# Retention attention with a token mixer on one core: another order of the work on all engines, other places for the scalings of v, and a last tile in halves

## The chip, the cores and the metric

The kernel runs on one core of a Trainium2 chip. A core has five engines that run side by side, each through its own list of instructions in order: TensorE (PE, matmuls, with its weight loads shown as PEld), VectorE (DVE), ScalarE (ACT), GpSimd (POOL) and SyncE (SP). They wait for each other by semaphores. Transfers are issued from SyncE's and GpSimd's lists and carried out by 16 DMA engines. Matmuls read SBUF and write PSUM, which here is used as eight banks; DVE and ACT carry results from PSUM to SBUF.

The metric is the device time of one execution in microseconds. Four runs of the kernel before gave 98.87, 99.43, 99.64 and 100.15, with a median of 99.54.

## The reference, cut to what matters

Four batches, eight heads, 768 positions, 64 features a head. The first stage is a causal attention without softmax, with a decay `lam` of its own for each head; the second mixes tokens and ends in a projection.

```python
for b in range(nb):                      # 12 blocks of 64 positions
    intra = (qb @ kb.T * Dmask) @ vb     # Dmask[i, j] = lam ** (i - j) for i >= j, else 0
    inter = (qb * lam_pow) @ kv_state    # lam_pow = lam ** (pos + 1)
    out[:, :, sl] = intra + inter
    kv_state = lam ** 64 * kv_state + (kb * rev_pow).T @ vb
x = out                                  # as (4, 768, 512), heads side by side
wq, wk = x @ w_q, x @ w_k                # 512 -> 64 each
W_tok = (wq @ wk.T) / 8                  # 768 x 768 for each batch
y = relu(W_tok @ x) @ w_out              # (4, 768, 512), float32
```

Inputs and output are float32; the kernel computes in bfloat16 with float32 sums in PSUM.

## The kernel before

The work is cut into 16 pairs of heads, n = 4 * batch + pair, and each pair into six chunks of 128 positions. As the decay is a power, it is split: q is multiplied by lam to the position (`Dq`), v is divided by it (`DvI`), and the mask is then a plain triangle.

The steps of a pair, by the names in the order string: q, k, v are loaded by GpSimd's queue, one transfer of 192 KB (as written) for each, with a cast (L111 to L121). `sv` scales v in place, on DVE (`:v`) or on GpSimd (`:p`) (L236). `Aq` and `Ak` transpose q and k on TensorE (L246, L257), twelve transposes each; `eq` brings q back with its decay on DVE, `ek` brings k back on DVE or ACT. `S0` and `S1` are the scores of three chunks each (L272). `M0` and `M1` multiply them by the mask on DVE, from PSUM; in their place `Mc` copies them on ACT and `Mm` masks the copy in SBUF on DVE. `P` makes the states between chunks (L314): for n under 6 in their whole form, where TensorE adds all earlier chunks into each state and `G` is one copy; for the others in a shorter form, where DVE adds in three instructions. `I` applies the states to q, `V` the masked scores to v, into the same banks. `ex` brings the result to `xnat`, `F` transposes it, `ef` (or two `eg`) brings that to `xT`.

When the four pairs of a batch are done, its mix follows: `Q` projects (or `Qp`, one pair at a time), `eQ` copies, `K` (or `Kh`) transposes and `eK` (`ek2`) copies, `Y` multiplies wk with x, `YA`, `YB`, `YC` copy, `m` applies wq, `em` (or two `eh`) takes the relu, `O` is the output projection of a tile of 128 tokens (four matmuls of 128x512), and `eo` copies that tile to one of 12 buffers and has SyncE store it. `Z.c` is c matmuls on a block of zeros, which nothing reads (L526); nine of them stand ahead of all.

```
    for word in ORDER.split():
        piece, _, eng = word.partition(":")
        piece, *banks = piece.split("@")
        name, *at = piece.split(".")
```

The order string (from L29) is all the planning that runs: the scheduler of the framework is off, and each engine's list is the words that fall to it, in the order of the string. `S0.5@2` is the scores of pair 5 into banks 2 and 3; `:a`, `:v` and `:p` name the engine. The string opens with GpSimd's words: its loads and its scalings. `hold.14` makes SyncE wait for k of pair 14 before it stores anything, so the stores do not meet most of the loads.

Of the kernel before, what the change touches and what calls it, by code (L numbers as in the profile page):

```python
# [9 lines left out]
BF16 = mybir.dt.bfloat16  # L10
F32 = mybir.dt.float32
ALU = mybir.AluOpType
ACT = mybir.ActivationFunctionType

B, H, S, D = 4, 8, 768, 64
CH = 128
NCH = S // CH
HD = H * D
DHY = 64
NP = H // 2  # L20
HALF = 3 * CH
N = B * NP
WHOLE = 6
# [6 lines left out]
q.2 k.2 v.2 q.3 k.3 v.3 wq.0 wk.0 q.4 k.4 v.4 wo.0 q.5 k.5 v.5 q.6 k.6 v.6 q.7 k.7 v.7 sv.4:p q.8  # L30
k.8 v.8 sv.5:p q.9 k.9 v.9 q.10 k.10 v.10 sv.7:p q.11 k.11 v.11 q.12 k.12 v.12 sv.9:p q.13 k.13
v.13 sv.10:p q.14 k.14 v.14 sv.11:p q.15 k.15 v.15 sv.12:p sv.13:p sv.14:p hold.14 Aq.0@0 dq.2
eq.0@0 dq.3 Z.5@7 Ak.0@0 dq.1 ek.0@0:v Z.3@7 S1.0@0 sv.0:v S0.0@2 Mc.0@2 M1.0@0 Z.3@7 P.0@4 Aq.1@5
G.0@4:a Mm.0:v Z.1@7 I.0@0 eq.1@5 Ak.1@4 V.0@0 ek.1@4:v ex.0@0:a S0.1@4 sv.1:v S1.1@2 Mc.1@4 Z.1@7
F.0@0 M1.1@2 P.1@1 ef.0@0:a Aq.2@4 Mm.1:v G.1@1:a eq.2@4 Z.1@7 Ak.2@0 I.1@2 ek.2@0:v V.1@2 S1.2@0
sv.2:v ex.1@2:a S0.2@4 Mc.2@4 M1.2@0 Z.3@7 P.2@2 Aq.3@3 G.2@2:a Mm.2:v F.1@4 eq.3@3 Ak.3@2
ef.1@4:v I.2@0 V.2@0 ek.3@2:v ex.2@0:a sv.3:v Z.1@7 S0.3@2 S1.3@4 cw.0:a M1.3@4 Mc.3@2 Z.2@7 P.3@0
Qp.0.0@1 F.2@6 G.3@0:a Mm.3:v Qp.0.1@1 ef.2@6:a I.3@4 V.3@4 Qp.1.0@0 ex.3@4:a Aq.4@6 Ak.4@7 eq.4@6
F.3@4 ek.4@7:a Qp.1.1@0 Qp.0.2@1 eg.3.0@4:v Qp.1.2@0 eg.3.1@4:v Qp.0.3@1 eQ.0.0@1:v Qp.1.3@0
S1.4@4 eQ.0.1@0:a Kh.0.0@1 M1.4@4 ek2.0.0@1:a Kh.0.1@0 S0.4@6 ek2.0.1@0:a M0.4@6 Y.0@0 YA.0@0:a  # L40
YB.0@0:v Aq.5@1 YC.0@0:a m.0.1@6@7 eq.5@1 m.0.0@4@5 eh.0.1.0@6:a eh.0.0.0@4:v eh.0.0.1@5:a Ak.5@1
eh.0.1.1@7:a m.0.2@4@6 ek.5@1:v m.0.3@5@0 eh.0.2.1@6:a eh.0.3.1@0:v S0.5@2 eh.0.3.0@5:a S1.5@6
eh.0.2.0@4:v P.4@0 O.0.5@5 G.4@0:v M1.5@6 I.4@0 eo.0.5@5:a V.4@0 M0.5@2 Aq.6@4 ex.4@0:a Ak.6@5
eq.6@4 O.0.4@6 ek.6@5:a sv.6:v S1.6@4 S0.6@0 M1.6@4 F.4@7 O.0.3@2 ef.4@7:a M0.6@0 P.5@3 eo.0.3@2:a
Ak.7@7 G.5@3:v Aq.7@0 ek.7@7:a P.6@2 eq.7@0 I.5@4 V.5@4 G.6@2:v S0.7@0 ex.5@4:a eo.0.4@6:v Aq.8@7
M0.7@0 I.6@2 S1.7@4 O.0.0@6 eq.8@7 M1.7@4 V.6@2 eo.0.0@6:a O.0.2@7 ex.6@2:a sv.8:v P.7@6
eo.0.2@7:a Ak.8@2 G.7@6:v P.8@3 ek.8@2:a F.5@7 G.8@3:v Aq.9@6 ef.5@7:a Ak.9@2 eq.9@6 S1.8@4
ek.9@2:a S0.8@0 I.7@6 M1.8@4 V.7@6 F.6@2 ex.7@6:a M0.8@0 O.0.1@3 ef.6@2:v F.7@6 eo.0.1@3:a Aq.10@7
ef.7@6:v S0.9@2 eq.10@7 S1.9@0 Ak.10@6 M1.9@0 Q.1.0@7 ek.10@6:a M0.9@2 Q.1.1@4 eQ.1.0@7:a I.8@6
eQ.1.1@4:a S1.10@0 P.9@5 M1.10@0 K.1@4 V.8@6 eK.1@4:a G.9@5:v Aq.11@2 ex.8@6:a Y.1@4 eq.11@2  # L50
Ak.11@5 YA.1@4:a YB.1@4:v S0.10@2 ek.11@5:v YC.1@4:a m.1.0@6 M0.10@2 em.1.0@6:a m.1.1@0 Aq.12@5
P.10@4 em.1.1@0:a eq.12@5 m.1.3@2 I.9@6 G.10@4:v em.1.3@2:a V.9@6 m.1.2@0 ex.9@6:v I.10@4
em.1.2@0:a F.8@2 V.10@4 ef.8@2:v S0.11@0 ex.10@4:a S1.11@6 M0.11@0 O.1.1@2 M1.11@6 F.9@3
eo.1.1@2:a O.1.0@0 ef.9@3:a Ak.12@2 eo.1.0@0:a P.11@3 ek.12@2:v Ak.13@1 Aq.13@0 G.11@3:v ek.13@1:a
S1.12@6 S0.12@4 eq.13@0 I.11@2 V.11@2 M0.12@4 O.1.4@0 ex.11@2:a M1.12@6 F.10@1 eo.1.4@0:a F.11@2
ef.10@1:a S0.13@6 ef.11@2:v S1.13@4 Ak.14@0 M1.13@4 P.13@1 ek.14@0:a Aq.14@2 G.13@1:v Q.2.0@3
eq.14@2 Q.2.1@0 eQ.2.0@3:a M0.13@6 S1.14@2 eQ.2.1@0:a I.13@4 O.1.5@1 M1.14@2 V.13@4 sv.15:v
eo.1.5@1:a P.14@0 ex.13@4:a Aq.15@2 G.14@0:v K.2@1 Ak.15@3 eK.2@1:a P.12@4 eq.15@2 P.15@0
ek.15@3:a Y.2@1 G.12@4:v G.15@0:v S0.14@4 YB.2@1:a S0.15@2 I.12@6 YA.2@1:a M0.14@4 V.12@6 YC.2@1:a
O.1.2@0 ex.12@6:a M0.15@2 S1.15@4 eo.1.2@0:a I.14@6 m.2.1@2 M1.15@4 F.12@1 em.2.1@2:a V.14@6  # L60
ef.12@1:a I.15@4 ex.14@6:v m.2.2@2 V.15@4 em.2.2@2:a F.13@0 ex.15@4:v F.14@1 ef.13@0:a m.2.0@2
m.2.3@6 ef.14@1:v F.15@4 em.2.0@2:a O.1.3@0 ef.15@4:v em.2.3@6:a Q.3.0@1 eo.1.3@0:a Q.3.1@6
eQ.3.0@1:a O.2.0@0 eQ.3.1@6:v K.3@1 eo.2.0@0:v O.2.4@6 eK.3@1:a Y.3@7 eo.2.4@6:a O.2.3@6 YA.3@7:v
YB.3@7:v YC.3@7:v m.3.1@0 eo.2.3@6:a O.2.2@4 em.3.1@0:a m.3.0@6 eo.2.2@4:a m.3.2@2 m.3.3@0
em.3.0@6:v O.2.5@5 em.3.2@2:a em.3.3@0:a O.2.1@4 eo.2.5@5:v O.3.0@0 eo.2.1@4:a O.3.2@1 eo.3.0@0:v
O.3.4@4 eo.3.2@1:a O.3.3@5 eo.3.4@4:v O.3.1@1 eo.3.3@5:a O.3.5@0 eo.3.1@1:a eo.3.5@0:a
# [4 lines left out]
def kernel(  # L71
# [11 lines left out]
    nc = tc.nc  # L83
# [73 lines left out]
    blank = consts.tile([128, HD], BF16, name="blank")  # L157
# [75 lines left out]
    def copy(eng, to, of):  # L233
        return (nc.scalar.copy if eng == "a" else nc.vector.tensor_copy)(out=to, in_=of)  # L234
# [28 lines left out]

    def turned_q(n, o):
        qT[n] = tsb.tile([128, S], BF16, tag="qT", name="qT")
        nc.vector.tensor_tensor(out=qT[n], in0=PSH[:, o, 0:S], in1=Dq[n % NP], op=ALU.mult)  # L266
# [33 lines left out]
    def whole(n):  # L300
        return n < WHOLE


    def drawn(n, o):
        pr[n, 0] = tsb.tile([128, 2, HALF], BF16, tag="pr0", name="pr")
        nc.scalar.copy(out=pr[n, 0], in_=PS[:, o : o + 2, 0:HALF])

    def masked_late(n, eng):
        of = pr[n, 0].rearrange("j l (c i) -> j l c i", c=3)
        (nc.gpsimd if eng == "p" else nc.vector).tensor_tensor(  # L310
            out=of, in0=of, in1=mask2, op=ALU.mult
        )

    def states(n, o):  # L314
        to = PS[:, o, 0 : (NCH - 1) * D].rearrange("e (c f) -> e c f", c=NCH - 1)
        for c in range(NCH - 1):
            end = 2 if c < 2 and not whole(n) else NCH - 1
            for hl in range(2):
                mm(  # L319
                    to[R[hl], c:end, :],  # L320
                    fk[n][:, hl, c, :],
                    vn[n][:, hl, c, :].unsqueeze(1).to_broadcast([128, end - c, D]),
                    start=(c == 0),
                    stop=(c == NCH - 2),
                    skip_group_check=True,
                )

    def summed(n, o, eng):
        gs[n] = tsb.tile([128, NCH - 1, D], BF16, tag="gs", name="gs")
        of = PS[:, o, 0 : (NCH - 1) * D].rearrange("e (c f) -> e c f", c=NCH - 1)  # L330
        if whole(n):
            copy(eng, gs[n], of)
            return
# [186 lines left out]

    held = consts.tile([1, D], BF16, name="held")
# [3 lines left out]

    def zeros(count, o):  # L526
        for _ in range(count):
            mm(PS[:, o, :], blank[:, 0:128], blank, start=True, stop=True)  # L528
# [6 lines left out]
        sv=scale_v, Aq=turn_q, Ak=turn_k, eq=turned_q, ek=turned_k, S0=scores(0), S1=scores(1),  # L535
        M0=masked(0), M1=masked(1), Mc=drawn, Mm=masked_late, P=states, G=summed, I=inter, V=values, ex=attended, F=flip,
# [39 lines left out]
```

## Time and profile before

| | us |
|---|---|
| median of four runs | 99.54 |
| profiled execution, its time | 99.35 |
| its span, first to last instruction | 97.6 |
| TensorE busy | 89.8 |
| DVE busy | 72.4 |
| ACT busy | 61.5 |
| GpSimd busy, issues of its transfers included | 61.5 |
| first matmul of pair 3's k | 18.94 |
| landing of the last load, v of pair 15 | 67.36 |
| start of the last tile's matmuls, O.3.5 | 92.50 |
| issue and landing of the last store | 94.22, 96.27 |

Rows of digits on the page cut the span into 40 slices of 2.44 us; a digit is the busy share in tenths. A row of the chain gives a start, a duration, and what ran. In a row of the timeline the brackets tell how long the engine was idle before it and what ended that. The granted clock of TensorE was 1.00 from 5.9 us on. Landings are read from the trace's record of each transfer's semaphore, and the starts of the pieces by laying the trace's matmuls, in order, against the order string (all 1469 are in the trace).

### The profile page before, as it was taken

How to read it: one execution, taken by the hardware profiler on the slowest of the kernel's cores; microseconds unless marked ns; L12 is line 12 of the kernel's file. 1: busy time of each engine (PE TensorE's matmuls, PEld its weight loads, DVE VectorE, ACT ScalarE, POOL GpSimd, SP SyncE). 2: the span in 40 equal slices, each digit the busy share in tenths (PEclk: the TensorE clock that was granted, in tenths of full speed). 3: DMA queues.
4: the chain of work that ended last, by engine and by line, in shares of the span. 5: the costliest groups of instructions: out<-in, count | busy, mean ns of one | idle time of the engine just before them, and what ended most of it. 6: DMA issues, size and time to landing. Idle time of an engine off the chain costs nothing.

```text
span 97.6 us, 3425 instructions
## 1 busy us (share of the span) xinstructions
PE 89.8 (92%) x1469; PEld 56.6 (58%) x1469; DVE 72.4 (74%) x140; ACT 61.5 (63%) x101; POOL 61.5 (63%) x65
## 2 busy tenths in 40 slices
PE   5999899899989999999899999999999999999930
PEld 1354666667555657677657685776696764434400
DVE  5738798893889999998798699689999835554200
ACT  5576294378548458379557596775589992593440
POOL 5999999599579999999999999980000000000000
PEclk9999999999999999999999999999999999999999
DMA  0999999999999999999999999999970202545782
GB/s 1 97 145 160 163 158 168 157 163 191 186 165 161 168 160 166 165 160 166 168 167 160 166 164 161 167 188 376 380 287 11 108 7 108 215 169 213 284 307 102
DMA packets 67438, 16.60 MB, mean 170 GB/s; under 512 B 63840, under 2 KB 64352, under 8 KB 67424
## 3 DMA queue, kind: packets, MB, share of 16 engines
q0 software_dynamic: 63792, 10.10, 140.1%
q1 hardware_dynamic: 3632, 6.30, 17.1%
q8 instruction: 11, 0.18, 0.7%
q14 instruction: 3, 0.02, 0.1%
HBM read 20.19 MB, written 6.29 MB: 271 GB/s over the span
## 4 chain that ended last, share of the span: by engine, by line
PE 69%; POOL 10%; DMA 8%; DVE 4%; ACT 3%; issue 2%; POOLq 0%; ACTq 0%
PE ps L508 22%; DMA fk<-in_k_dram 8%; PE ps L359 6%; PE ps L277 6%; PE ps L382 5%; PE ps L260 5%; PE ps L319 5%; PE ps L404 4%; PE ps L251 4%; POOL fq L113 3%; PE ps L455 3%; POOL fk L117 3%; POOL fv L121 3%; PE ps L347 3%; PE ps L479 2%
## 5 line engine op out<-in xcount | busy, mean ns | idle before, releaser
L291 DVE TENSOR_TENSOR pr<-ps,mask 128x768 bf16<-128x768 f32 x28 | 26.0, 950 | 0.8 <-PE ps L277 0.7
L508 PE MATMUL ps<-wo,rmT 128*128 128x512 bf16 x96 | 23.6, 380 | 0.0
L117 POOL DMA_DIRECT2D fk<-in_k_dram x16 | 16.7, 1041 | 1.4 <-DMA wo<-in_moe_w_out_dram 1.4
L234 ACT COPY osb<-ps 128x512 f32<-128x512 f32 x19 | 11.2, 589 | 10.0 <-PE ps L508 9.8
L121 POOL DMA_DIRECT2D fv<-in_v_dram x16 | 16.7, 1046 | 0.3 <-issue 0.3
L234 ACT CAST xnat<-ps 128x768 bf16<-128x768 f32 x13 | 10.4, 800 | 7.2 <-PE ps L359 6.9
L113 POOL DMA_DIRECT2D fq<-in_q_dram x16 | 14.1, 880 | 1.3 <-POOLq L560 0.8
L239 POOL TENSOR_TENSOR fv<-fv,DvI 128x768 bf16<-128x768 bf16 x9 | 13.4, 1506 | 0.0
L508 PEld LDWEIGHTS <-rmT 128*128 128x128 bf16 x96 | 8.3, 98 | 8.6 <-issue 0.7
L528 PE MATMUL ps<-blank 128*128 128x512 bf16 x29 | 9.9, 460 | 1.2 <-DVE blank L158 1.2
L266 DVE TENSOR_TENSOR qT<-ps,dq 128x768 bf16<-128x768 bf16 x16 | 8.9, 554 | 2.7 <-PE ps L251 2.4
L490 ACT ACTIVATE rmT<-ps 128x768 bf16<-128x768 f32 (+1 forms) x16 | 10.6, 721 | 0.2
L277 PE MATMUL ps<-qT,kT 64*128 64x128 bf16 x192 | 9.0, 218 | 0.4 <-DVE kT L234 0.3
L234 ACT COPY kT<-ps 128x768 bf16<-128x768 bf16 x9 | 7.2, 800 | 2.9 <-PE ps L260 2.4
L359 PE MATMUL ps<-fv,pr 128*128 128x64 bf16 x192 | 8.5, 194 | 0.5 <-issue 0.5
L260 PE MATMUL ps<-ident,fk 128*64 128x128 bf16 x192 | 8.3, 221 | 0.6 <-DMA fk<-in_k_dram 0.5
L251 PE MATMUL ps<-ident,fq 128*64 128x128 bf16 x192 | 8.6, 227 | 0.1
L319 PE MATMUL ps<-fv,fk 128*64 128x128 bf16 (+4 forms) x160 | 8.0, 229 | 0.0
L277 PEld LDWEIGHTS <-kT 64*128 64x128 bf16 x192 | 5.6, 94 | 4.0 <-DVE kT L234 1.4
L382 PE MATMUL ps<-order,xnat 128*128 128x128 bf16 x96 | 7.8, 220 | 0.0
L359 PEld LDWEIGHTS <-pr 128*128 128x128 bf16 x192 | 6.8, 98 | 1.8 <-issue 0.8
L260 PEld LDWEIGHTS <-fk 128*64 128x64 bf16 x192 | 6.2, 110 | 2.6 <-DMA fk<-in_k_dram 1.2
(68 smaller groups left out, 130.6 us busy)
## 6 DMA issues: line engine op xcount, KB each, us to landing
out_dram<-osb SPq DMA_DIRECT2D x24, 256.0 KB, 2.0
fq<-in_q_dram POOLq DMA_DIRECT2D x16, 192.0 KB, 7.5
fk<-in_k_dram POOLq DMA_DIRECT2D x16, 192.0 KB, 8.0
fv<-in_v_dram POOLq DMA_DIRECT2D x16, 192.0 KB, 8.1
wo<-in_moe_w_out_dram POOLq DMA_DIRECT2D x1, 512.0 KB, 8.8
wqk<-in_moe_w_q_dram POOLq DMA_DIRECT2D x1, 64.0 KB, 7.2
wqk<-in_moe_w_k_dram POOLq DMA_DIRECT2D x1, 64.0 KB, 6.9
lam_all<-in_lam_dram SPq DMA_DIRECT2D x1, 4.0 KB, 2.5
```

Of the source, the lines that this page charges most:

```text
L113: nc.gpsimd.dma_start(out=fq[n], in_=rows_q(n))
L117: nc.gpsimd.dma_start(out=fk[n], in_=rows(n, k))
L121: nc.gpsimd.dma_start(out=fv[n], in_=rows(n, v))
L234: return (nc.scalar.copy if eng == "a" else nc.vector.tensor_copy)(out=to, in_=of)
L239: (nc.gpsimd if eng == "p" else nc.vector).tensor_tensor(out=vn[n], in0=fv[n], in1=DvI[:, 2 * kk : 2 * kk + 2, :].unsqueeze(3).to_broadcas ...
L260: nc.tensor.transpose(PSH[R[hl], o, c * CH : (c + 1) * CH], fk[n][:, hl, c, :], ident)
L277: mm(PS[:, o + hl, cc * CH : (cc + 1) * CH], kT[n][R[hl], c], qT[n][R[hl], c], start=True, stop=True, skip_group_check=True,)
L291: nc.vector.tensor_tensor(out=pr[n, a].rearrange("j l (c i) -> j l c i", c=3), in0=PS[:, o : o + 2, 0:HALF].rearrange("j l (c i) -> j l c ...
L319: mm(to[R[hl], c:end, :], fk[n][:, hl, c, :], vn[n][:, hl, c, :].unsqueeze(1).to_broadcast([128, end - c, D]), start=(c == 0), stop=(c == ...
L359: mm(PS[:, o + hl, c * D : (c + 1) * D], pr[n, c // 3][:, hl, (c % 3) * CH : (c % 3 + 1) * CH], vn[n][:, hl, c, :], start=False, stop=(c = ...
L382: nc.tensor.transpose(PSH[:, o, c * CH : (c + 1) * CH], xnat[b][:, c, kk * CH : (kk + 1) * CH], order,)
L508: mm(PS[:, o, :], rmT[b][:, kt].rearrange("f n i -> f (n i)")[:, t * CH : (t + 1) * CH], wo[:, kt, :], start=(kt == 0), stop=(kt == 3),)
```

## The change

It has five parts.

1. The order string is another one, for all engines. On TensorE pieces of several pairs stand closer together: for example Ak.15 and Aq.15 come ahead of S0.13, and four O of batch 0 stand between Y.1 and the m of batch 1. Evacuations change engine: DVE copies 14 output tiles instead of 5, ACT 9 instead of 19.
2. GpSimd's list: `wo`, the transfer of the output weights (512 KB as written), moves from behind v.4 to behind k.10. Eleven v are scaled there instead of nine (4, 5, 6, 8 to 15), at other places between the loads; DVE scales 0 to 3 and 7 instead of 0 to 3, 6, 8 and 15. The order is made so that no two scalings, one on each engine, run at once.
3. Which form a pair takes is now a word of the string: `Pw` is the whole form of P and `Gp` the DVE additions; the whole form is used for pairs 0 to 4, 6, 7 and 14. `Mc` and `Mm` take either half of the scores and are used eight times instead of four.
4. The zeros are float32: `Z.c` becomes one matmul for each four units, with 128 columns a unit. There are 32 units in 11 matmuls instead of 29 in 29 matmuls; three units fewer stand after Ak.3 and six more ahead of it.
5. The last batch's tile 5 is computed, copied and stored in two halves of 256 columns (`Oh`, `oh`), the first one before O.3.2, the second one last.

Four more functions (`turn_q4`, `turn_k4` and their evacuations) are added that no word of the string calls.

```diff
-WHOLE = 6
-    blank = consts.tile([128, HD], BF16, name="blank")
+    blank = consts.tile([128, CH], F32, name="blank")
...
-    def drawn(n, o):
-        pr[n, 0] = tsb.tile([128, 2, HALF], BF16, tag="pr0", name="pr")
-        nc.scalar.copy(out=pr[n, 0], in_=PS[:, o : o + 2, 0:HALF])
+    def drawn(a, n, o):
+        pr[n, a] = tsb.tile([128, 2, HALF], BF16, tag=f"pr{a}", name="pr")
+        nc.scalar.copy(out=pr[n, a], in_=PS[:, o : o + 2, 0:HALF])
...
-            end = 2 if c < 2 and not whole(n) else NCH - 1
+                end = 2 if c < 2 and not whole else NCH - 1
...
+    def mix_o_half(b, t, half, o):
+        at = slice(half * 256, (half + 1) * 256)
+        for kt in range(4):
+            mm(
+                PS[:, o, 0:256],
+                rmT[b][:, kt].rearrange("f n i -> f (n i)")[:, t * CH : (t + 1) * CH],
+                wo[:, kt, at],
+                start=(kt == 0),
+                stop=(kt == 3),
+            )
+
+    def mixed_o_half(b, t, half, o, eng):
+        at = slice(half * 256, (half + 1) * 256)
+        osb = outp.tile([128, HD], F32, tag="osb", name="osb")
+        copy(eng, osb[:, 0:256], PS[:, o, 0:256])
+        nc.sync.dma_start(out=out[b, t * CH : (t + 1) * CH, at], in_=osb[:, 0:256])
...
     def zeros(count, o):
-        for _ in range(count):
-            mm(PS[:, o, :], blank[:, 0:128], blank, start=True, stop=True)
+        while count > 0:
+            n = min(count, 4) * CH
+            mm(PS[:, o, 0:n], blank, blank[:, 0:1].to_broadcast([128, n]), start=True, stop=True)
+            count -= 4
```

GpSimd's words, before and after:

```diff
-q.2 k.2 v.2 q.3 k.3 v.3 wq.0 wk.0 q.4 k.4 v.4 wo.0 q.5 k.5 v.5 q.6 k.6 v.6 q.7 k.7 v.7 sv.4:p q.8
-k.8 v.8 sv.5:p q.9 k.9 v.9 q.10 k.10 v.10 sv.7:p q.11 k.11 v.11 q.12 k.12 v.12 sv.9:p q.13 k.13
-v.13 sv.10:p q.14 k.14 v.14 sv.11:p q.15 k.15 v.15 sv.12:p sv.13:p sv.14:p hold.14
+q.2 k.2 v.2 q.3 k.3 v.3 wq.0 wk.0 q.4 k.4 v.4 q.5 k.5 v.5 q.6 k.6 v.6 q.7 k.7 sv.4:p v.7 sv.5:p
+q.8 k.8 v.8 sv.6:p q.9 k.9 v.9 q.10 k.10 wo.0 sv.8:p v.10 q.11 sv.9:p k.11 v.11 q.12 k.12 v.12
+sv.10:p q.13 sv.11:p k.13 v.13 q.14 k.14 v.14 q.15 k.15 sv.12:p v.15 sv.14:p sv.13:p sv.15:p
+hold.14
```

TensorE's words after, from pair 3's k on, with engines and banks left out:

```
Ak.3 I.2 V.2 S1.3 S0.3 Pw.3 F.2 Aq.4 I.3 Qp.0.0 V.3 Qp.0.1 Ak.4 Qp.0.2 Qp.1.0 F.3 Qp.1.1 Qp.1.2
S0.4 S1.4 Qp.1.3 Qp.0.3 Ak.5 Aq.5 Kh.0.1 Kh.0.0 Pw.4 S1.5 S0.5 Y.0 I.4 Aq.6 Ak.6 P.5 m.0.1 m.0.3
V.4 S1.6 I.5 Aq.7 S0.6 m.0.0 Ak.7 V.5 F.4 S0.7 Pw.6 S1.7 Pw.7 Aq.8 m.0.2 I.7 I.6 Ak.8 V.6 V.7 F.5
Aq.9 F.6 F.7 S0.8 S1.8 Q.1.1 Q.1.0 Ak.9 P.8 K.1 Aq.10 Ak.10 P.9 Y.1 S0.9 I.8 S0.10 V.8 O.0.5 O.0.3
O.0.1 O.0.2 P.10 m.1.3 S1.10 m.1.1 F.8 O.0.0 m.1.0 S1.9 m.1.2 Aq.12 Aq.11 Ak.11 P.11 Ak.12 O.1.2
S0.11 I.10 I.9 O.1.1 V.10 O.1.4 V.9 O.0.4 S0.12 I.11 S1.11 O.1.5 F.10 V.11 F.9 O.1.0 F.11 P.12 Ak.14
Aq.13 Ak.13 Aq.15 Ak.15 Aq.14 P.13 S0.13 S1.13 Q.2.0 Q.2.1 S1.12 S1.15 I.13 P.15 K.2 V.13 S0.14
S0.15 Y.2 Pw.14 I.15 S1.14 I.12 V.12 V.15 m.2.3 I.14 V.14 F.12 F.15 F.13 F.14 m.2.0 m.2.2 m.2.1
O.1.3 Q.3.1 Q.3.0 O.2.4 K.3 O.2.2 Y.3 O.2.5 m.3.0 m.3.3 m.3.1 O.2.3 m.3.2 O.2.1 O.2.0 O.3.0 Oh.3.5.1
O.3.2 O.3.1 O.3.3 O.3.4 Oh.3.5.0
```

## The prediction

> **What bounds the kernel now.** I read the page first: busy shares, slices, the chain that ended last. Then GpSimd's timeline with the landings of its transfers, and last the starts of all matmuls against the order string.
>
> ```profile
> PE 89.8 (92%) x1469; PEld 56.6 (58%) x1469; DVE 72.4 (74%) x140; ACT 61.5 (63%) x101; POOL 61.5 (63%) x65
> PE   5999899899989999999899999999999999999930
> DVE  5738798893889999998798699689999835554200
> DMA  0999999999999999999999999999970202545782
> PE 69%; POOL 10%; DMA 8%; DVE 4%; ACT 3%; issue 2%; POOLq 0%; ACTq 0%
> ```
>
> TensorE is busy from 5 us on, but the DMA engines are as full until slice 29 (68 us). The input stream is a second bound beside TensorE, and DVE stands at 9 in the middle. The chain says where the one hands over to the other:
>
> ```profile
> 10.92 7.98 DMA fk<-in_k_dram
> 18.90 0.04 issue
> 18.94 0.53 PE ps L260 x12
> ...
> 26.67 0.55 ACT wkn L234 x2
> ...
> 28.14 0.38 ACT YA L234
> ...
> 28.55 0.43 DVE YB L234
> ...
> 29.00 0.57 DVE qT L266
> ```
>
> Until 18.94 the path is the arrival of k.3; after it TensorE, with other engines in it mostly at 25.7 to 31 (batch 0's mix). So I need two sums: TensorE's work after k.3, and the times at which the inputs of that work land.
>
> **TensorE's work, priced.** The spacing from the start of a piece's first matmul to that of the next piece repeats closely where nothing waits: Aq, Ak and F 0.335 us, S0 and S1 0.17, P 0.254, its whole form (Pw) 0.436, I 0.156, V 0.35, Q 0.65, Y 0.676, an m 0.162, an O 0.863, a zero 0.216. It is 0.098 longer where the next piece uses the array in another shape (64 output partitions, 64 contraction rows, all of it): O then O 0.863, O then a transpose 0.957. Before, from k.3's transposes on, these give 68.94 us with 78 switches of shape. The trace takes 74.43 (18.94 to 93.37). The other 5.49 are waits: 0.83 up to 27.26, 1.40 up to 31.39, 1.25 up to 49.82, 1.21 up to 57.43, 0.80 after that.
>
> After, the same prices give 67.87: eight fewer switches (-0.78), three fewer zeros past this point (-0.65), two more whole-form P (+0.36). That is -1.07, and it counts only if waits do not take it back.
>
> **GpSimd's list and the landings.**
>
> ```profile
> 17.95 0.76 POOL L140 DMA_DIRECT2D wo<-in_moe_w_out_dram  x1 [0.59 <-DMA fq<-in_q_dram]
> 19.18 0.82 POOL L113 DMA_DIRECT2D fq<-in_q_dram  x1 [0.47 <-DMA fk<-in_k_dram]
> ...
> 27.08 1.02 POOL L117 DMA_DIRECT2D fk<-in_k_dram  x1 [1.39 <-DMA wo<-in_moe_w_out_dram]
> ```
>
> These issues wait, each for the eighth transfer before it (q.3 landed at 17.66, k.3 at 18.89, wo at 26.79). The stream itself sets the pace: by the trace's landings 1.1 to 1.5 us a load, and 2.34 us for wo (24.45 to 26.79). The change moves wo from behind v.4 to behind k.10. So q.5 to k.10 land 2.34 us earlier (k.5 29.32 to 26.98, k.10 47.99 to 45.65), wo at about 47.99, and v.10 and later as now.
>
> GpSimd gets two more scalings, 1.506 us each, and eight instead of six stand before v.15. From the issue rows (0.85 to 1.05) I get v.15 issued at 61.9, not 60.05, with 5 us to its landing at 67.4, so the stream is not starved. The scaled v come just in time: sv.4 done at 27.45 (P.4 at 28.0 at the earliest), sv.10 at 51.2 (P.10 at 51.5), sv.15 at 68.9 (P.15 at 69.9). Cost 0, and up to about 0.5 where a landing slips.
>
> Now lay the new TensorE order, without waits, from 18.94. It runs ahead of the stream: k.5 wanted at 25.33 (1.65 too early), k.7 at 31.56 (2.83), k.10 at 41.02 (4.63), wo at O.0.5, 43.32 (4.67), k.15 at 61.72 (4.37). Waits in the earlier part, such as those of batch 0's mix, vanish in this lead. But at least 4.67 us of idle time stand by O.0.5, and 43.49 us of work are left: TensorE ends at 91.48 or later, against 93.37.
>
> **Other parts.** *Zeros in fp32.* 32 units, not 29, in 11 matmuls; no row shows an fp32 matmul. The row for 128x512 bf16 is 0.216 warm. The Trainium skill (FP8 and Floating Point Precision, TensorE Precision Notes) says true fp32 takes four passes through the array, so 128 fp32 columns would last what 512 bf16 do now. By the row a Z.4 costs 0.22, by the rule 0.86, an estimate; I take the rule. Past k.2's transposes (14.76) the rule puts k.3's at 19.0, as its landing does. Unhidden weight loads on each pass (0.111 each) could add 0.9; the 1.65 us of lead at k.5 hides that. With no cover it costs those 0.9, or gains nothing, since k.3 has to land.
>
> *Scaling by both engines.* One DVE scaling met one of GpSimd's:
>
> ```profile
> L239 POOL TENSOR_TENSOR fv<-fv,DvI x9: 1485/1506/1528, 29.4 to 63.9; 128x768 bf16<-128x768 bf16 x9
> L239 DVE TENSOR_TENSOR fv<-fv,DvI x7: 948/958/1467, 8.2 to 69.8; 128x768 bf16<-128x768 bf16 x7
> ```
>
> The longest (at 34.65, GpSimd's running until 35.29) took 0.51 us extra; GpSimd lost nothing. So the ban returns 0.5 us of DVE, once. The Trainium skill (SBUF — State Buffer, Who interferes with whom) calls this an exclusive lock: a DVE instruction with two SBUF inputs waits out one of GpSimd's that reads SBUF. That speaks against the change, for the late masks (Mm, 0.551 us, both inputs in SBUF) grow from 4 to 8, five of them while GpSimd scales for 16.6 of some 43 us. By the row this is 5 x 0.39 x 0.51 = 1.0 us of DVE, by the rule (half of 1.506 each) 1.5. I take the row, and 0.2 of it on the path.
>
> *Evacuations.* By row means DVE's work from k.3 to the first Q.3 is 58.7 us (before 57.7), ACT's within 1 us of before. From O.0.5 to Q.3.1 DVE has 30.9, less 53 ns of overlap per instruction (57.7 summed was 52.5 busy), so 28.1, against 29.54 on TensorE: 95%. Before, Q.1.0 to Q.3.0, it was 94%.
>
> *The last tile in halves.* The last copy falls from 0.589 to about 0.37 us. But SyncE needs 0.333 us for each issue, and the 0.69 us DVE copy of O.3.4 ends at the same moment: that tile's store goes first, the half's at 0.70 us after the last matmul instead of 0.68. What may remain is the smaller store: 0 to 0.25 us of 2.05. I take 0.1. SyncE also holds all stores until k.14 has landed (62.7); eleven copies come before that instead of eight, of 12 buffers, so none waits for one.
>
> **Likeliest.** After 49.82 before waited 2.01 us, of which 1.11 around batch 1's mix (Y.1, m.1.0, m.1.1, P.10). The new order puts four O (3.5 us) and P.10 between Y.1 and m.1.3 as cover. That leaves 0.8 of such waits plus 0.2: TensorE ends at 92.5, 0.87 earlier, 0.97 with the tail. The profiled execution took 99.35 for its span of 97.6; carried to the median of 99.54 it is **98.5**. Chance 0.45, alone 97.4 to 99.3.
>
> **Rivals.** *DVE keeps the old waits* (0.3): after O.0.5 TensorE again waits 2.0 us or a little less. 91.48 + 2.0 = 93.5, so 99.5. For it: 95% load on DVE; the gain in TensorE's sum then only pays for waiting on wo. Against it: the cover at batch 1's mix.
>
> *DVE binds behind k.15* (0.2, slower). From Ak.15 to Q.3.1 DVE has 13.2 us by means, 11.9 net, over TensorE's 11.14. At the 91% that DVE reached in its densest stretch (11.23 of 12.33 us, 27.26 to 39.59) that is 13.1, a wait of 1.9; with 1.65 between O.0.5 and k.15, as before had, and 0.15 at the end, TensorE ends at 95.2: 101.2. It decides once k.15's transposes start later than 68.3 us, for 25.1 us of work are left from there. Before they started at 71.0 with less left.
>
> *The stream does not move up* (0.05): GpSimd, with sv.4 to sv.6 earlier, limits it, the change doing less than it says. Then wo lands 2.34 later still and the end is 93.8 + 1.0: 100.8. Against it: five us and more between issue and landing.
>
> **Range and chances.** 97.4 (no wait after O.0.5, full tail) to 100.9. A measurement of this kernel tells about 1% from no change. Of the likeliest case nearly all but a third, with a little of the rival at 99.5, lies below 98.54; the rest to 100.54 is the same; the last two rivals are slower: 0.43, 0.35, 0.22.
>
> **What will show it.** k.5's transposes near 27.0, k.10's near 45.7, O.0.5 near 48, held by DMA; k.15's before 68; Q.3.1 near 78.5; the last matmul near 92.5. Wrong if wo lands much off 48, if DVE is over 92% busy from 66 to 79, or if fp32 zeros delay k.3's transposes by over 1.5 us.

## The result: no measurable change, and the profile after

The kernel after took 99.69 us in the median of 36 runs (98.95 to 101.84), the kernel before, run beside it, 99.64 in 55 (98.86 to 100.41). The ratio is 1.0002, with a 95% interval of 0.9984 to 1.0021. The prediction was 98.5. Here and below, medians are of all executions, and ratios leave out those more than 1.5% above the fastest of the same kernel. The profiled execution took 99.68 for its span of 97.9 (before: 99.35 for 97.6).

The rows of the page that answer to those shown of before, busy shares, slices and the chain:

```profile
PE 89.0 (91%) x1466; PEld 58.0 (59%) x1466; DVE 77.5 (79%) x146; ACT 57.7 (59%) x94; POOL 64.5 (66%) x67
PE   5999999989876998989999999999999999999910
DVE  5737999997799899787896997977999975872520
DMA  0999999999999999999999999999993013346880
POOL 44%; DMA 23%; PE 21%; ACT 5%; issue 3%; DVE 0%; POOLq 0%
```

TensorE now has holes from 24 to 32 us (8, 7, 6, where before stood 9, 8, 9), and few later. DVE has more to do. The chain no longer runs through TensorE for 69% of the span but through the input stream, GpSimd and the transfers, for 67%. In order of time, the chain shows where the stream hands over, and how the kernel ends:

```profile
60.11 7.19 DMA fk<-in_k_dram
67.30 0.04 issue
67.34 0.53 PE ps L260 x12
...
75.97 1.40 PE ps L426 x24
...
89.40 3.45 PE ps L552 x16
92.86 0.45 PE ps L569 x4
```

Until 67.30 the path is the arrival of k.15. After that it is mostly TensorE to 93.3, with copies on ACT in between from 70.8 to 75 and copies of batch 3's mix, on ACT and DVE, from 83.2 to 84.5. The waits for a landing are at the transposes of k.5, as predicted, and of k.6 (the prediction named k.7). The rows of its timeline (start, duration, and in brackets the idle time before and what ended it):

```profile
27.37 0.53 PE L260 MATMUL ps<-ident,fk 128*64 128x128 bf16 x12 [0.73 <-DMA fk<-in_k_dram]
...
31.75 0.53 PE L260 MATMUL ps<-ident,fk 128*64 128x128 bf16 x12 [0.74 <-DMA fk<-in_k_dram]
```

Busy times by stretch (length, then TensorE, its weight loads, DVE, ACT, GpSimd, the granted clock, the DMA share and GB/s):

```profile
27.30:45.00 17.70, 16.02 (x354) 12.11 (x356) 16.54 (x28) 11.87 (x22) 17.68 (x17) 1.00 2.19 166
66.00:79.00 13.00, 12.77 (x298) 10.10 (x293) 12.21 (x25) 12.16 (x21) 3.37 (x3) 1.00 0.77 237
```

From 27.3 to 45 us TensorE lacks 1.7 us; from 66 to 79 it lacks 0.23, with DVE at 94%. So TensorE came out a little ahead: its last matmul ended at 93.29, before at 93.53. But the last store landed at 96.69, before at 96.27. From TensorE's end to the last landing the kernel before needs 2.74 us, the kernel after 3.40. The issues of the last three stores (number, KB each, median us from issue to landing), first in the kernel before:

```profile
out_dram<-osb SPq DMA_DIRECT2D x3, 256.0 KB, 2.0
```

and in the kernel after:

```profile
out_dram<-osb SPq DMA_DIRECT2D x2, 256.0 KB, 2.6
out_dram<-osb SPq DMA_DIRECT2D x1, 128.0 KB, 2.6
```

The half-size store takes as long as the whole ones (2.51, 2.71 and 2.60 us; before 2.04, 2.05 and 2.05). The stretch from 90 to 98 us has one more row of transfers in the kernel after that the kernel before does not have:

```profile
q14 instruction: 1, 0.01, 0.2%
```

That is one packet of an instruction fetch, a transfer that brings an engine the next piece of its list (then MB, and the share of 16 engines): 8192 bytes, at 94.62 us by the trace's record of transfers. In the kernel before the last one comes at 98.19, after the last store. This was the first lead.

### The profile page after: what moved, and what is told of

Its sections match the earlier page's. It is cut to its first block, busy times and chain, and to the rows that moved or that the text cites. A ratio compares the mean times of both kernels' runs of the same rounds, so it can differ in the third digit from the quotient of the medians.

```text
span 97.9 us, 3422 instructions
## 1 busy us (share of the span) xinstructions
PE 89.0 (91%) x1466; PEld 58.0 (59%) x1466; DVE 77.5 (79%) x146; ACT 57.7 (59%) x94; POOL 64.5 (66%) x67
## 4 chain that ended last, share of the span: by engine, by line
POOL 44%; DMA 23%; PE 21%; ACT 5%; issue 3%; DVE 0%; POOLq 0%
POOL fk L117 12%; POOL fv L121 11%; POOL fq L113 10%; PE ps L552 10%; POOL fv L239 9%; DMA fq<-in_q_dram 8%; DMA fk<-in_k_dram 7%; DMA fv<-in_v_dram 7%; PE ps L448 3%; PE ps L523 2%; PE ps L426 1%; ACT pr L344 1%; PE ps L318 1%; PE ps L569 1%; PE ps L499 1%
## 5 line engine op out<-in xcount | busy, mean ns | idle before, releaser
L332 DVE TENSOR_TENSOR pr<-ps,mask 128x768 bf16<-128x768 f32 x24 | 22.4, 950 | 0.5 <-PE ps L318 0.3
L552 PE MATMUL ps<-wo,rmT 128*128 128x512 bf16 x92 | 22.5, 380 | 0.0
L239 POOL TENSOR_TENSOR fv<-fv,DvI 128x768 bf16<-128x768 bf16 x11 | 16.4, 1498 | 2.8 <-DMA fv<-in_v_dram 2.8
L234 DVE COPY osb<-ps 128x512 f32<-128x512 f32 x14 | 9.7, 689 | 5.7 <-PE ps L552 5.5
L234 ACT COPY osb<-ps 128x512 f32<-128x512 f32 (+1 forms) x11 | 6.0, 547 | 11.7 <-PE ps L552 8.5
L234 ACT COPY kT<-ps 128x768 bf16<-128x768 bf16 x12 | 9.4, 801 | 4.9 <-PE ps L260 4.9
L592 PE MATMUL ps<-blank 128*128 128x512 f32 (+3 forms) x22 | 11.0, 612 | 1.1 <-DVE blank L158 1.1
L234 ACT CAST xnat<-ps 128x768 bf16<-128x768 f32 x11 | 8.8, 804 | 3.0 <-PE ps L403 2.8
L344 ACT CAST pr<-ps 128x768 bf16<-128x768 f32 x8 | 6.4, 801 | 6.1 <-PE ps L318 6.1
L534 ACT ACTIVATE rmT<-ps 128x768 bf16<-128x768 f32 (+1 forms) x11 | 7.5, 725 | 1.7 <-PE ps L523 1.6
```

The source lines that it names most:

```text
L239: (nc.gpsimd if eng == "p" else nc.vector).tensor_tensor(out=vn[n], in0=fv[n], in1=DvI[:, 2 * kk : 2 * kk + 2, :].unsqueeze(3).to_broadcas ...
L332: nc.vector.tensor_tensor(out=pr[n, a].rearrange("j l (c i) -> j l c i", c=3), in0=PS[:, o : o + 2, 0:HALF].rearrange("j l (c i) -> j l c ...
L552: mm(PS[:, o, :], rmT[b][:, kt].rearrange("f n i -> f (n i)")[:, t * CH : (t + 1) * CH], wo[:, kt, :], start=(kt == 0), stop=(kt == 3),)
L592: mm(PS[:, o, 0:n], blank, blank[:, 0:1].to_broadcast([128, n]), start=True, stop=True)
```

## The experiments

Theory at the start: the earlier stream and the cover at batch 1's mix make TensorE faster, as predicted, and the tail gives it back. The rivals: the stream is not what limits (another order of loads would change nothing); the halves themselves make the tail slow; the float32 zeros cost the time.

### The load of wo: the stream limits this order, not the other

In the kernel after, wo moves back to where it was:

```diff
-q.4 k.4 v.4 q.5 ... k.10 wo.0 sv.8:p
+q.4 k.4 v.4 wo.0 q.5 ... k.10 sv.8:p
```

> The changed kernel with wo back behind v.4 in GpSimd's list, nothing else. Theory (the new order runs ahead of the input stream, and TensorE's waits up to 46 us are for it): q.5 to k.10 land 2.3 us later, k.5's transposes go from 27.4 to 29.7, k.6's from 31.8 to 34, O.0.5 from 48.5 to about 50.5, and the time grows by about 2 us to 101.7, ratio 1.02. Rival (those waits are for copies on DVE and ACT): the later landings are taken up by waits that are there anyway, at most 0.5 us more, ratio under 1.006.

Measured: 103.15 us in the median of four runs; the ratio of 1.0281 (1.0222 to 1.034) is from the two at 102.06 and 102.68. The profiled one took 103.62. There the transposes of k.5 waited 3.44 us for their landing at 29.93, and what followed ran at half clock, which was not expected. TensorE's timeline, the page's clock row, and a window of that stretch:

```profile
29.97 0.85 PE L260 MATMUL ps<-ident,fk 128*64 128x128 bf16 x12 [3.44 <-DMA fk<-in_k_dram]
```

```profile
PEclk9999999999975599999999999999999999999998
```

```profile
29.16:35.99 6.83, 6.02 (x98) 4.97 (x100) 3.17 (x6) 1.85 (x4) 6.81 (x7) 0.50 2.24 164
```

From 29.16 to 35.99 the granted clock was 0.50; twelve transposes take 0.85 us in place of 0.53. k.5's transposes start 2.60 us later than in the kernel after, as its landing does; by k.10's it is 4.27 (50.29 against 46.02), and the rest came with the half clock. So the order of the kernel after needs wo late, and at k.5 the stream sets its pace: that step of the prediction holds.

The counterpart takes the order of before, with the last tile in halves (as in the second run of the next part), and moves wo by one group of loads:

```diff
-q.4 k.4 v.4 wo.0 q.5 k.5 v.5 q.6
+q.4 k.4 v.4 q.5 k.5 v.5 wo.0 q.6
```

> The order of the kernel before on all engines, with the last tile in halves as in the earlier run of that, and the output weights' load moved from behind v.4 to behind v.5 alone. k.5 should land near 27.0 and the load of the weights near 30.5, ahead of O.0.5. Theory of the prediction (in the order of before TensorE is not ahead of the stream, so an earlier stream is worth nothing unless the order uses it): k.5's transposes stand behind batch 0's mix in TensorE's list, so they move by 0.3 us at most, and the time is that of the halves alone, 99.3, within 0.3 us. Rival (the earlier stream itself gains): 0.8 us or more, to 98.5.

Measured: ratio 0.9974 (0.994 to 1.0008), against 0.998 (0.9946 to 1.0014) for the halves alone. k.5 landed at 27.36 instead of 29.32, its transposes started at 29.89 instead of 29.61. To an order that does not use it, the earlier stream brought nothing that can be measured.

### The halves

The kernel after with its last tile whole:

```diff
-Oh.3.5.1@5 ... oh.3.5.1@5:a ... Oh.3.5.0@7 eo.3.4@5:v oh.3.5.0@7:a
+O.3.5@7 eo.3.4@5:v eo.3.5@7:a
```

> The changed kernel with its last tile whole again, computed last, one ACT copy and one store. In the changed kernel's profile the last store landed 3.4 us after TensorE's end, in the one before 2.9 us. Theory (the half's store and that of the tile ahead of it come 0.43 us apart and hold each other up): 0.3 to 0.5 us less than the changed kernel, 99.3, ratio to before about 0.996, and the last store landing 2.9 us after TensorE's end. Rival (slow stores in that one execution, the halves are worth nothing either way): 99.6 to 99.8, ratio 1.000.

Measured: ratio 0.9974 (0.9944 to 1.0003). The last three stores took 2.73, 2.48 and 2.30 us, with the fetch at 93.46, and TensorE's end to the last landing took 2.99. (The expectation's 2.9 us for the kernel before count from 93.37, TensorE's end by the prices; from its last record they are 2.74.) So the stores are long without the halves too. In this order the whole tile still saves 0.41 us of tail: the fetch stands at TensorE's end and not 1.33 us behind it, and the last store, issued 0.71 after it, takes 2.30 and not 2.60.

The kernel before with its last tile in halves:

```diff
-O.3.2@1 ... O.3.5@0 ... eo.3.5@0:a
+Oh.3.5.1@6 O.3.2@1 ... Oh.3.5.0@0 ... oh.3.5.0@0:a
```

> The kernel before, with its last tile alone in two halves, the first ahead of O.3.2, the second last. Theory (halves cost time): 0.3 to 0.5 us more, ratio 1.003 to 1.005. Rival (worth nothing): 1.000. What the prediction had: 0.1 us less, 0.999.

Measured: ratio 0.998 (0.9946 to 1.0014). The last store took 2.00 us, and TensorE's end to its landing 2.68, against 2.74. That the halves slow the tail falls; where the stores are not disturbed they save the predicted little.

### Fewer loads

The kernel after without the eleven loads of q from pair 5 on, in whose place it reads an earlier pair's q (this part of the computation is left out, so that the stream is shorter):

```diff
 def load_q(n):
+    if n > 4:
+        fq[n] = fq[n % 4]
+        return
```

> The changed kernel without the loads of q for pairs 5 to 15 (they use q of pair n mod 4, so that output isn't the reference's); all work on the engines stays, the input stream is 11 of 51 transfers shorter. Theory (stream): of the 4.3 us that TensorE waits between k.3's transposes and 46 us about 2 go, time 97.3 to 98. Rival (waits between the engines): within 0.6 us of the changed kernel, 99.1 to 99.7.

Measured: 98.78, 102.87, 103.01 and 103.04 us. The profiled one (103.04) shows why the longer ones say nothing on the stream. In TensorE's timeline, and in a window behind it:

```profile
39.67 0.57 PE L362 MATMUL ps<-fv,fk 128*64 128x320 bf16 x9 [1.77 <-DVE fv L242]
```

```profile
41.20:44.60 3.40, 3.30 (x57) 2.74 (x51) 2.08 (x5) 1.55 (x2) 3.40 (x5) 0.50 1.88 172
```

DVE's scaling of v.7 took 2.22 us, from 37.40 on, beside one of GpSimd's (37.00 to 38.80), TensorE idled 1.77 us, and 1.5 us later the clock fell to 0.50 for 3.4 us. This run changed more than it should have and is inconclusive: the one run at 98.78 lies between what the two theories expected.

### The zeros

The kernel after with zeros in bfloat16, 512 columns a unit:

```diff
-    while count > 0:
-        n = min(count, 4) * CH
-        mm(PS[:, o, 0:n], blank, blank[:, 0:1].to_broadcast([128, n]), start=True, stop=True)
-        count -= 4
+    for _ in range(count):
+        mm(PS[:, o, :], blank[:, 0:128], blank, start=True, stop=True)
```

> The kernel after with its zeros in bfloat16, 512 columns a unit, one matmul for each unit as in the kernel before; nothing else changed. Theory (four passes): a float32 unit of 128 columns costs about what a bfloat16 unit of 512 columns does, 0.24 against 0.216 us, so k.3's transposes stay within 0.3 us of 19.51, the time within 0.2 us of the kernel after (99.7), and each zero unit shows as one matmul of about 0.22 us. Rival (the float32 zeros are what makes k.3's transposes late and costs the end): k.3's transposes return to 19.0 and the time falls by about 0.5 us, to 99.2.

Measured: ratio 0.9993 (0.9968 to 1.0018), no difference from the kernel after. The groups of zeros in the kernel after (count, then busy us and mean ns of one):

```profile
L592 PE MATMUL ps<-blank 128*128 128x512 f32 x8 | 6.0, 867 | 1.1 <-DVE blank L158 1.1
```

Each float32 zero word of up to four units is two matmuls there, and from its first matmul to the next piece a Z.4 takes 1.01 us, a Z.3 0.85, a Z.2 0.63 (a switch of shape included), about 0.24 a unit. In this run the bfloat16 words take 0.96, 0.75 and 0.54. k.3's transposes start at 19.15 with bfloat16 zeros, 0.07 after their landing, and at 19.44 to 19.51 in three traces with float32 zeros, 0.2 to 0.65 after it. The delay is gone at k.5: there TensorE waits 1.04 us beyond its price with the bfloat16 zeros and 0.34 to 0.80 with the others.

### The fetch: moving it with instructions that do nothing

In the traces so far an 8 KB fetch stands within 1.3 us of DVE's 192nd record (semaphore waits and drains counted). The kernel before has 192 such records in all, the kernel after 195. So memsets of one column on DVE should move it. First the kernel before, with six at the start, where DVE waits:

```diff
+    spare = consts.tile([128, 1], F32, name="spare")
...
+    for _ in range(6):
+        nc.vector.memset(spare, 0.0)
     for word in ORDER.split():
```

> The kernel before with six memsets of one column more on DVE, at the start where DVE waits for ACT, so that DVE runs as many instructions (146) as in the kernel after. Theory (an instruction fetch of DVE's list falls beside the last stores): the fetch of 8 KB that came after the last store (98.19 us) moves ahead of it, to 93 to 96 us, at least one of the last three stores takes 2.3 to 2.7 us to land instead of 2.05, TensorE's end stays within 0.2 us of 93.4, and the time rises by 0.2 to 0.5 us, to about 100.0. Rival (the slow last stores belong to the order of the kernel after): all last stores land in 2.0 to 2.1 us and the time is that of the kernel before, 99.6.

Measured: the fetch moved from 98.19 to 90.82. Stores issued at 89.01 and 90.83 took 2.42 and 2.38 us, but the last three 2.05 to 2.07: it was too early for the last ones. The ratio was 0.9936 (0.9914 to 0.9958), faster, which neither theory had expected.

The kernel after with 24 at the same place:

> The kernel after with 24 memsets of one column more on DVE at the same place, so that a fetch tied to the count of DVE's instructions comes 24 instructions earlier, near 83 us. Theory (fetch): the fetch shows between 80 and 88 us, the last three stores land in 2.0 to 2.1 us instead of 2.5 to 2.7, and the time falls by about 0.5 us, to 99.2. The memsets may cost at the start: if the first q is multiplied later than before, up to 0.3 us of the gain goes. Rival (order): the last stores still take 2.5 to 2.7 us and the time is 99.7 or a little more.

Measured: the fetch came at 80.43, and the last three stores took 2.03, 2.04 and 1.98 us. But the time rose, ratio 1.0077 (1.0049 to 1.0104), for in the timeline of DVE the memsets held up the first q:

```profile
5.32 2.83 DVE L608 MEMSET spare<- 128x1 f32 x23
8.19 0.55 DVE L308 TENSOR_TENSOR qT<-ps,dq 128x768 bf16<-128x768 bf16 x1
```

The first q is multiplied at 8.19 instead of 5.84. The tail says fetch; the time is that of a late start. So the next run has ten of them, as a word `idle.10` behind eq.0, where DVE waited 1.48 us:

```diff
-eq.0@0 dq.3
+eq.0@0 idle.10 dq.3
```

> The kernel after with ten memsets of one column on DVE behind eq.0, where DVE waited 1.47 us for TensorE (6.40 to 7.87). In every trace so far the last 8 KB fetch came as DVE's 192nd listed instruction was reached, so it should come ten DVE instructions earlier, between 87 and 92 us, and not at 94.62. Theory (the fetch lengthens the stores that are in flight with it, and the last ones decide the end): the last two stores land in 2.0 to 2.2 us instead of 2.6 to 2.7, TensorE's end stays within 0.3 us of 93.3, and the time falls by 0.4 to 0.6 us, to 99.2. Rival (the gain of the six memsets in the kernel before has another cause): the stores shorten but the time stays at 99.7.

Measured: 98.56 us in the median, ratio 0.9934 (0.9909 to 0.9958). The fetch came at 86.65, the last three stores took 2.04, 2.04 and 1.98.

### What else do the memsets do?

Six memsets had made the kernel before faster too, where the fetch had not lain beside its last stores. The same six late, behind ef.15, in the kernel before:

```diff
-ef.15@4:v
+ef.15@4:v idle.6
```

> The kernel before with the same six memsets on DVE, but behind ef.15, where DVE waits for over a microsecond (79.16 to 80.77), and not at the start. Theory A (the count of DVE's instructions made the run with six memsets at the start 0.6 us faster): the last fetch comes near 91 us as there, and the time is 99.1. Theory B (their place at the start made it, by shifting the first pieces): the last fetch comes near 91 us too, and the time is that of the kernel before, 99.6.

Measured: ratio 0.9952 (0.9928 to 0.9975), the fetch at 90.32. It is not the place at the start. With the halves and six at the start (`Oh` as above, the six as above):

> The kernel before with the last tile in halves and six memsets on DVE at the start, both as in the earlier runs of each. If the two gains (0.2 and 0.6 us) are of separate causes, they add up: 98.9, and the last store lands 0.2 us earlier than with the memsets alone. If they are one (where the end of the kernel stands against the last fetch), the time is 99.1 as with the memsets alone.

Measured: ratio 0.9936 (0.9914 to 0.9958). Beside the next run, on the same chip and without the halves (0.9966), this does not tell one gain from two. The kernel before with six at the start once more, unchanged:

> The kernel before with six memsets on DVE at the start once more, for a second trace and a second set of runs, since the first trace had a time (99.37) in the upper fifth of its own runs. If the gain is real, the median is 99.1 again and this trace shows where it is: either waits of TensorE from 18.94 to 50 us, 3.4 in the kernel before, are below 2.9 us, or k.3 lands before 18.7. If not, the median is 99.5 to 99.7.

Measured: ratio 0.9966 (0.9943 to 0.999), so the gain is there. In this trace k.3 landed at 18.61 and TensorE ended at 92.76; 14 matmul records are missing, and its waits can't be summed.

What these runs had in common besides the count is an added tile of 4 bytes on each partition, which shifts the places of others. So the memsets went into a tile that the kernel has:

```diff
-    spare = consts.tile([128, 1], F32, name="spare")
...
-        nc.vector.memset(spare, 0.0)
+        nc.vector.memset(one, 1.0)
```

> The kernel before with six memsets more on DVE at the start, as in the earlier runs, but written into a tile that the kernel has already (one), so that no tile is added and every tile keeps its place in SBUF. Theory A (the count of DVE's instructions makes the kernel before faster by 0.35 to 0.6 us): the last fetch comes near 90.5 us and the ratio to the kernel before is 0.993 to 0.997. Theory B (the added tile shifts the places of the others, and with them the loads): the fetch moves in the same way and the ratio is 1.000 within 0.002.

Measured: ratio 1.002 (0.999 to 1.0051), the fetch at 90.33. With the same six instructions and no new tile the gain of the kernel before is gone. A second trace of the kernel before, unchanged:

> The kernel before once more, for a second trace. If its last fetch again comes after the last store (near 98 us) and the last stores again take 2.0 to 2.1 us, then its stores are not what the six memsets improve, and the difference must lie in the time from k.3's landing to the last tile (73.6 us in the first trace; 73.5, 73.8 and 73.1 in those with memsets) or in k.3's landing itself.

Measured: 99.32 us, the fetch again at 98.18, the last three stores 2.02, 2.06 and 2.05 us, and TensorE's end at 93.53, as in the first trace, though k.3 had landed at 18.52 and not at 18.90. So neither the stores nor k.3's landing explain what the runs with the tile gained. The tile with a single memset:

> The kernel before with the added tile of one column (spare, 4 bytes on each partition) and one memset of it on DVE. The last fetch should still come after the last store (97 us or later). Theory (the places of the tiles): the ratio to the kernel before is 0.993 to 0.997, as in the four runs that had the tile and six memsets. Rival (it takes six DVE instructions and the tile together): 1.000 within 0.002.

Measured: ratio 0.9972 (0.9938 to 1.0006), the fetch at 97.03. It lies with the runs that had the tile, but its interval reaches 1. That the added tile gives the kernel before 0.3 to 0.6% is likely; how it does is not shown.

### The deciding pair, and the order of before with a fetch at its end

Ten memsets in the kernel after, with no tile added (the edit is shown against the run with `idle.10`), beside the kernel after itself, on one chip:

```diff
-    spare = consts.tile([128, 1], F32, name="spare")
...
-            nc.vector.memset(spare, 0.0)
+            nc.vector.memset(one, 1.0)
```

> The kernel after with ten memsets more on DVE behind eq.0, written into a tile that the kernel has already, so that no tile is added. Theory A (the fetch beside the last stores costs the kernel after 0.5 to 0.6 us): the last fetch comes near 86.7 us, the last stores land in 2.0 to 2.1 us, and the ratio to the kernel before is 0.993 to 0.996, as with the added tile (0.9934). Theory B (the gain came from the places of the tiles): the stores shorten too, but the ratio is above 0.997.

> The kernel after once more, on the same chip as the run with the ten memsets, for a second trace and a direct comparison. Expected by the theory of the fetch: the last fetch beside the last stores again (94 to 95 us), at least two of the last three stores above 2.4 us, and a ratio to the kernel before of 1.000 within 0.003. If the last stores take 2.0 to 2.1 us here although the fetch lies beside them, the fetch is not the cause.

Measured: with the ten memsets 98.89 us (98.41 to 101.24), ratio 0.9934 (0.9908 to 0.9961); the kernel after 99.64 (98.76 to 100.69), ratio 0.9998 (0.9971 to 1.0025). The last three stores with the memsets:

```profile
out_dram<-osb SPq DMA_DIRECT2D x2, 256.0 KB, 2.0
out_dram<-osb SPq DMA_DIRECT2D x1, 128.0 KB, 2.0
```

and in the second trace of the kernel after:

```profile
out_dram<-osb SPq DMA_DIRECT2D x2, 256.0 KB, 2.6
out_dram<-osb SPq DMA_DIRECT2D x1, 128.0 KB, 2.6
```

At last the order of before, its last copy on DVE and two memsets more (into `one`), to bring the fetch to its last stores:

```diff
-eo.3.5@0:a
+eo.3.5@0:v
```

> The kernel before with its last copy on DVE instead of ACT (0.69 against 0.59 us) and two memsets more on DVE into a tile it has already, so that DVE's 192nd listed instruction is about the last copy and the last fetch comes near 94.5 to 95.5 us, beside the last stores, as in the kernel after. Theory (fetch): the last store or the last two take 2.3 to 2.7 us, and from TensorE's end to the last landing it is 3.2 to 3.5 us, not 2.74; with the slower copy the ratio is 1.004 to 1.007. Rival (the order of the kernel after makes its stores slow): the last stores take 2.0 to 2.1 us, from TensorE's end to the last landing it is 2.85 us, and the ratio is 1.001.

Measured: the fetch came at 92.94, earlier than meant. The stores issued at 91.08, 92.00, 92.80 and 93.67 took 2.47, 2.72, 2.53 and 2.30 us; the one issued last, at 94.59, took 2.04, and so the tail was 2.80 us. So the ratio of 1.0026 (0.9998 to 1.0053) is not that of a long last store; it is near the 1.002 of the six memsets into `one`. The fetch and the two stores in its midst:

```profile
q14 instruction: 1, 0.01, 1.0%
...
out_dram<-osb SPq DMA_DIRECT2D x2, 256.0 KB, 2.6
```

The long stores follow the fetch into the order of before. The runs that bear on the tail, which is the time from TensorE's end to the last landing:

| kernel | DVE's records | last fetch, us | last three stores, us | tail, us | ratio |
|---|---|---|---|---|---|
| before | 192 | 98.19 | 2.04, 2.05, 2.05 | 2.74 | 1 |
| before, six into `one` | 198 | 90.33 | 2.04, 2.05, 2.05 | 2.74 | 1.002 |
| before, DVE's last copy, two into `one` | 196 | 92.94 | 2.53, 2.30, 2.04 | 2.80 | 1.0026 |
| after | 195 | 94.62 | 2.51, 2.71, 2.60 | 3.40 | 1.0002 |
| after again | 195 | 93.70 | 2.51, 2.72, 2.60 | 3.40 | 0.9998 |
| after, last tile whole | 195 | 93.46 | 2.73, 2.48, 2.30 | 2.99 | 0.9974 |
| after, ten into `spare` | 204 | 86.65 | 2.04, 2.04, 1.98 | 2.78 | 0.9934 |
| after, ten into `one` | 204 | 86.87 | 2.04, 2.03, 1.97 | 2.77 | 0.9934 |
| after, 24 into `spare` | 219 | 80.43 | 2.03, 2.04, 1.98 | 2.78 | 1.0077 |

Three more traces of the order of after without added instructions (bfloat16 zeros, wo early, fewer loads) have the fetch 1.3 us behind TensorE's end and tails of 3.40, 3.41 and 3.40 us.

In the dense end of the kernel a store issued from about 1.9 us before the fetch to 0.7 after it takes 0.1 to 0.7 us longer; near 86.7 us, where the stores are further apart, only 0.1. The record of single packets shows how a last store comes to be late. It is 128 packets of 1,024 bytes. In the kernel after, 120 of them had ended by 95.71, and eight followed between 95.96 and 96.26; with the ten memsets into `one` all 128 ended between 94.95 and 95.44. Packets of 2,048 bytes mostly take 85 ns there, but the four that lead up to the fetch, each ending within 20 ns of the next one's start, took 124 to 162, the fetch itself 309, and two behind it 280 and 227. Eight of 128 is the share of one of the 16 DMA engines, so it seems that one engine falls behind and the whole store waits for it; that it is one engine is inferred. The second trace of the kernel after has the same picture, eight packets from 95.04 to 95.34 behind 120 that had ended by 94.78.

Ten instructions that compute nothing take 0.63 us from the tail of the kernel after (3.40 to 2.77) and 0.64% from its time (0.9998 to 0.9934). The kernel after with the ten memsets beats both kernels.

## Why the prediction was wrong

**The failed step is the tail.** The prediction said of the halves "What may remain is the smaller store: 0 to 0.25 us of 2.05. I take 0.1", so it let each store's 2.05 us stand as a constant. That term measured +0.66 us (2.74 to 3.40), not -0.1. With the fetch out of the way it is +0.03 (2.77 with the ten memsets): the half's store takes 1.97 in place of 2.05, but is issued 0.80 us after TensorE's end, not the 0.70 of the prediction (0.69 before). The halves alone gave -0.06 in the kernel before (2.68 against 2.74), within the range given. The other 0.63 us is the fetch of DVE's list, which the change moved from behind the last store into its flight by three more records on DVE. The prediction counted what DVE's instructions cost in time, and not what their number triggers.

**TensorE's sum and its idle time: right in kind, a size off.** wo landed at 47.98 for a forecast of 47.99, k.10 at 45.41 for 45.65, k.5 at 27.33 for 26.98; k.5's transposes were held by DMA, and k.15's started at 67.34, before the 68.3 from which the slower rival decides. O.0.5 started at 48.41, not held by wo, which had landed 0.43 us earlier: TensorE itself was late. By the prices it had idled 5.1 us since 18.94, for a forecast of 4.67, but only 2.3 of that stand at the landings of k.3, k.5 and k.6. The rest is small waits in the other pieces, so those of the earlier part did not vanish in the lead, as the prediction had it. From O.0.5 on the price of 43.49 met 1.2 us of waits for a forecast of 1.0; the kernel before had paid 2.0 (the last record ends 0.16 us past the priced end, before and after). The gain at TensorE's end, forecast at 0.87 us, was 0.24 in the first trace, 0.50 with the ten memsets into `one` and 1.15 in the second trace, the fastest of its 22 runs. It goes with the start of O.0.5 (48.41, 48.20, 47.60), for the waits behind it were 1.1 to 1.2 us in all three; the second trace had k.5 and k.6 earlier, and no wait at k.6. The ratio of 0.9934, where the tail is undisturbed, puts it at about 0.65 us. So of a forecast of 0.97 about 0.65 came, and the tail took as much back. (99.54 less 0.97 is 98.57; the prediction's 98.5 is rounded down.)

**The stream.** It was said not to be starved. k.15 landed at 67.30 for 66.10 before: in the chain the scaling of v.11 on GpSimd waits for its landing (until 52.91), and k.13 is issued only at 54.45. The 1.2 us cost TensorE 0.33 at most, as it was only just there.

**The rivals.** "DVE keeps the old waits" gave the nearest time, 99.5, for a wrong reason: after O.0.5 the waits fell from 2.0 to 1.2. "DVE binds behind k.15" did not come, though DVE was at 94% from 66 to 79 us, over the 92% that was to prove the forecast wrong: TensorE lacked 0.23 us there. In the kernel before DVE was at 96% in the same stretch and TensorE lacked 0.03:

```profile
66.00:79.00 13.00, 12.97 (x275) 9.37 (x270) 12.50 (x26) 10.40 (x19) 0.00 (x0) 1.00 0.60 216
```

A busy share of an engine beside TensorE is not a wait. "The stream does not move up" fell with the landing of wo.

**Smaller steps.** The zeros: a Z.4 came to 0.91 us without the switch of shape, where the rule of four passes gave 0.86 and the row 0.22, and the lead at k.5 covered the delay, as said. Scaling by both engines: no DVE scaling was lengthened any more, and of the late masks one of eight met a GpSimd scaling and lost 0.82 us, not five with 0.39 x 0.51 each. The groups of the tiles (shortest, median and longest in ns, then from when to when):

```profile
L239 POOL TENSOR_TENSOR fv<-fv,DvI x11: 1462/1497/1536, 26.5 to 68.6; 128x768 bf16<-128x768 bf16 x11
L239 DVE TENSOR_TENSOR fv<-fv,DvI x5: 947/951/959, 8.6 to 36.4; 128x768 bf16<-128x768 bf16 x5
L348 DVE TENSOR_TENSOR pr<-pr,mask x8: 548/549/1369, 11.4 to 73.6; 128x768 bf16<-128x768 bf16 x8
```

The sum was 0.82 for a forecast of 1.0, close by chance. The one mask fits the Trainium skill's rule of waiting it out (SBUF — State Buffer, Who interferes with whom) better than the 0.51 of the row before. It started at 27.12, the scaling of v.4 ended at 28.07, and the mask at 28.49. The rule makes it 28.07 plus 0.55, 28.62; the row makes it 27.12 plus 0.55 plus 0.51, 28.18. The scaling behind the row's 0.51 tells the same: it started at 34.65, GpSimd's ended at 35.29, and it ended 0.82 later, for the 0.95 that it takes alone. So the loss is no constant. It is what is left of GpSimd's scaling, less 0.12, and the prediction took the row where the rule was nearer; its sum came out near because one mask met a scaling, and not five.

## What to carry to other kernels

Price the end of a kernel by its own rows, and ask of each transfer there what else can be in flight with it, fetches of instructions too. If a change leaves the last stores longer than the same stores before, look at the transfers that are not yours before you look at the order; a handful of idle instructions on the engine whose list is fetched can show it. A gain on the bounding engine counts only as far as the tail passes it on, and an engine's busy share says little about who waits for it.

## What the runs showed of the hardware

- Fetches of DVE's list, 8192 bytes each, come near its 71st record (68th to 76th in all traces but that with 24 memsets, where it was the 61st) and at its 191st to 193rd, about 120 apart. The Trainium skill (Runtime: NRT & Kernel Launch, Instruction fetch mechanics) speaks of blocks of 16 KiB and of a cost that is mostly hidden. The trace of the kernel after has eleven fetches of 16,384 bytes and four of 8192; DVE's are of 8192, and the one beside the last stores cost 0.63 us. Why packets next to a fetch of 0.31 us take up to 280 ns in place of 85 is not shown.
- A DVE instruction with both inputs in SBUF that met a scaling on GpSimd ended its own time, less 0.12 us, behind the end of that scaling: a scaling of v (0.95 alone) 0.82 behind it, a mask (0.55 alone) 0.42. So it was in 25 of the 30 meetings in the traces here. In three the two overlapped by 0.11 us or less and nothing was lost; two, in the run with fewer loads, do not fit. The same mask lost 0.12 us in one trace and 1.53 in another.
- In the run with wo early the granted clock fell to 0.50 at 29.16, 2.6 us into a wait of 3.44 us, and stayed there for 6.83 us. In the run with fewer loads it fell at 41.20, 1.5 us behind a wait of 1.77 us (TensorE was busy 1.78 of the 3 us from 36 to 39), and stayed for 3.4 us. Waits of up to 1.46 us at k.5 (the kernel after with its last tile whole) left it at 1.00.
- Adding a tile of 4 bytes on each partition, which nothing reads, went with 0.3 to 0.6% less time in five experiments on the kernel before (in four the interval lies below 1; one of them had the halves too), and with none in the kernel after (0.9934 with the tile and without). The cause is open.
